# The first pair of W_in chunks of blocks 1 and 2 in seven products of half the depth

## The chip, the cores and the metric

The kernel runs on one core of one Trainium2 chip. The metric is device time in microseconds (us) of one execution, from the first to the last instruction of the core and what lies around them. Engines are named as in the profile: PE is TensorE's matmul, PEld its weight load, DVE is VectorE, ACT is ScalarE, POOL is GpSimd, SP is the queue that issues DMAs.

## The reference

Attention over 16 heads of 576 positions with a cumulative bias, a gated layer with RMS norm, and a second layer. The change lies in the second layer, cut here to what matters:

```python
def _moe2_ref(x, w_in, w_out):            # x: 1152 x 512, w_in: 512 x 2048, w_out: 2048 x 512
    h = x @ w_in
    sp = np.where(h > 20.0, h, np.log1p(np.exp(np.minimum(h, 20.0))))
    g = h * np.tanh(sp)                   # Mish
    return (g @ w_out)
```

## The kernel before

The 1152 tokens are three blocks (0, 1, 2) of 384 columns. Each fp32 operand is split into a high and a low part (`split_pair`: ScalarE copies the high part, VectorE subtracts it to get the low one), and each product is three passes (`PASS`) over these parts. `xh` and `xl` hold the two parts of x, four chunks of 128 rows each.

The 2048 columns of `w_in` are 16 chunks in eight pairs, g = 0 to 7. For one block and one pair there are two ways to compute h:

- **plain**, `h2_mm(b, g)`: two chunks, four row chunks, three passes, 24 matmuls of 384 columns into one pair of PSUM banks (`banksS`, two such pairs exist). Then `mish(b, g)` on ScalarE writes the tile `u`, `mish_split(b, g)` splits it into one half of the tile `glb`, and `out_mm(b, g)` multiplies by `w_out` (18 matmuls of 512 columns), adding up over g.
- **seven products**, `strassen(g, gaps)`: blocks 1 and 2 together. Strassen's scheme (in Winograd's form) takes seven products of half the depth (`product`, six matmuls each) in place of eight, 42 matmuls in place of 48. It needs sums of quarters of x, which are made once (`t_sums(1)` to `t_sums(4)`, split by `t_split`), and sums of quarters of the pair's weights, made for each g (`s_restore` adds high and low parts into a tile c, `s_sums` does four additions in it, `s_hi` on ScalarE and `s_lo` on VectorE split it). The seven products are, in order: a (needs no sum), b (needs `s_lo` and x sum 2), c (x sum 3), d (x sum 1), a again, c again (x sum 4), d again. The last three add onto the PSUM bank of a first one, after `add` has read it. `gaps` holds work that is written between the products.

The program's order on each engine is the order of the calls; each engine works strictly in that order. Block 0 goes plainly for all g, in a loop in which `out_mm(0, g - 2)` follows `h2_mm(0, g)`, and each step ends in two calls of `w_tick`. A `w_tick` decodes one tile of packed fp64 weights into high and low parts: loads through SP into tiles `r0` to `r3`, three operations on ScalarE, three on VectorE; a load can start when the tile four places earlier has been decoded.

After the loop pair 0 of blocks 1 and 2 goes plainly, `h2_mm(2, 0)` and `h2_mm(1, 0)`, around `out_mm(0, 7)`; pairs 1 to 7 go by `strassen`, each followed by `out_mm(1, g - 1)`. Three orders matter for what waits on what: `mish_split(0, g)` writes half g % 2 of `glb`, which `out_mm(0, g - 2)` reads; x's sum 1 and 2 are written over block 0's part of `xh` and `xl`, sum 3 over block 2's, sum 4 into half 0 of `glb`; sums and weights share the tiles `r0` to `r3`, `mm`, `ring4` and `ring8` by tag. The order after the loop:

```python
    out_mm(0, NG - 2)
    mish_split(0, NG - 1)
    t_split(4)
    s_restore(1)
    s_sums(1)
    h2_mm(2, 0)
```

Of the kernel before, what the change touches and what calls it, by code (L numbers as in the profile page):

```python
# [7 lines left out]
F32 = mybir.dt.float32  # L8
# [4 lines left out]
ALU = mybir.AluOpType  # L13
# [29 lines left out]
def tile_kernel(ctx: ExitStack, tc: tile.TileContext, kq, qq, v, s, w1, w2, rms_g, out):  # L43
# [10 lines left out]
    def sbt(shape, dt, tag, name):  # L54
        return sb.tile(shape, dt, tag=tag, name=name)
# [352 lines left out]
    def w_tick():  # L408

        n = done["c"]  # L410
        if n >= NUW or not free(seq[n]):
            return
        w_loads(LIM[0])
        done["t"] += 1
        ready = done["b"] > n
        if ready:
            w_hi(n)
        else:
            w_tops(n)
        for m in range(done["b"], min(n + 2, done["a"])):  # L420
            w_b(m)
            done["b"] = m + 1
        if n < done["b"]:
            w_c(n, not ready)
            done["c"] = n + 1
        if ready:
            w_tops(n)
        w_loads(LIM[0])
# [278 lines left out]

        add(o, quarter(0, c, b).bitcast(F32), quarter(1, c, b).bitcast(F32))

    def split_pair(h, l, src):  # L710
        nc.scalar.copy(out=h, in_=src)  # L711
        nc.vector.tensor_tensor(out=l, in0=src, in1=h.bitcast(F32), op=ALU.subtract)  # L712

    def product(t, A, B, start):
        n = 0
# [121 lines left out]
    def h2_mm(b, g):  # L837
        t = banksS()
        h2_t[b, g] = t
        for x in range(2):  # L840
            w = unit2(2 * (2 * g + x))
            n = 0
            for c in range(KD):
                for a, r in PASS:
                    nc.tensor.matmul(t[:, x, 0:TB], w[:, a, 128 * c:128 * c + 128],  # L845
                                     xhl[r][:, c, TB * b:TB * b + TB], start=(n == 0), stop=(n == 11))
                    n += 1
# [4 lines left out]
    def pair(t):  # L852
        return t[:, 0:2 * TB].rearrange("p (x n) -> p x n", x=2)
# [3 lines left out]
    def u_at(b, g):  # L857

        if (b, g) in u_t:
            return u_t[b, g]  # L860
        if b == 2 and g > 3:
            if not ub:
                ub.append(sbt([128, 4, 2, TB], F32, "w11", "ub"))
            u_t[b, g] = ub[0][:, g - 4]
        else:
            tag = ("mm", "ring8", "ring6", "ring0")[g] if b == 2 else ("hA", "hB")[g % 2] if b else                 ("hA", "hB", "mm")[g % 3]
            u_t[b, g] = sbt([128, 2, TB], F32, tag, "u")
        return u_t[b, g]

    def mish(b, g):  # L870
        nc.scalar.activation(out=u_at(b, g), in_=h2_t.pop((b, g))[:, :, 0:TB], func=ACTF.Mish)

    def mish_split(b, g):
        if not glb:
            glb.append(sbt([128, 2, 2, 2, TB], F32R, "w6", "glb"))
        g2_t[b, g] = gl = glb[0][:, g % 2 if b == 0 else (g + 1) % 2 if b == 2 else g < NG - 1]
        split_pair(gl[:, 0], gl[:, 1], u_t.pop((b, g)))
# [18 lines left out]
    def out_evac(b):  # L896
        for tt in range(TB // 128):
            if b == 0 and tt < 2:
                if not ob:
                    ob.append(sbt([128, 2, 512], F32, "r0", "osb"))  # L900
                t = ob[0][:, tt]
            else:
                t = sbt([128, 512], F32, f"r{(2 * b + tt) % 4}" if b else "hB", "osb")
            rows = slice(b * TB + 128 * tt, b * TB + 128 * tt + 128)

            cols = (slice(0, 256), slice(256, 512)) if (b, tt) == (NB - 1, 2) else (slice(0, 512),)
            for n, cs in enumerate(cols):
                if (tt + n) % 2 == 0:
                    nc.scalar.copy(out=t[:, cs], in_=o_t[b][tt][:, cs])
                else:  # L910
                    nc.vector.tensor_copy(out=t[:, cs], in_=o_t[b][tt][:, cs])
                nc.sync.dma_start(out=out[rows, cs], in_=t[:, cs])
# [3 lines left out]
    def t_sums(n):  # L916

        if n == 0:
            tq[0] = pair(sbt([128, 896], F32, "mm", "t0"))
        o = tq[0]  # L920
        if n:
            tq[n] = t = pair(sbt([128, 1024], F32, ("r2", "r3", "r0", "r1")[n - 1], f"t{n}"))
        if n == 0:
            restore(o, 0, 2)
        elif n == 1:
            restore(t, 0, 1)
            add(t, o, t, ALU.subtract)
        elif n == 2:
            restore(t, 1, 2)
        elif n == 3:  # L930
            add(t, tq[2], o, ALU.subtract)
            add(tq[2], tq[2], tq[1], ALU.subtract)
        else:
            restore(o, 1, 1)
            add(t, o, tq[2], ALU.subtract)

    def t_split(n):
        tsum[n] = ((quarter(0, 0, 0), quarter(1, 0, 0)), (quarter(0, 1, 0), quarter(1, 1, 0)),
                   (quarter(0, 0, 2), quarter(1, 0, 2)), (glb[0][:, 0, 0], glb[0][:, 0, 1]))[n - 1]
        split_pair(*tsum[n], tq[n])  # L940

    def s_restore(g):

        c_t[g] = sbt([128, 1024], F32, "r1", "c")
        for x in range(2):
            w = unit2(4 * g + 2 * x).bitcast(F32)
            add(c_t[g][:, 512 * x:512 * x + 512], w[:, 0], w[:, 1])

    def s_sums(g):

        a11, a12, a21, a22 = (c_t[g][:, 256 * n:256 * n + 256] for n in range(4))
        for o, x, y, op in ((a22, a21, a22, ALU.add), (a21, a11, a21, ALU.subtract),
                            (a11, a22, a11, ALU.subtract), (a12, a12, a11, ALU.subtract)):
            add(o, x, y, op)

    def s_hi(g):
        s_t[g] = [sbt([128, 1024], F32R, t, f"s_{t}") for t in (("r0", "ring4"), ("r2", "r3"))[g % 2]]
        nc.scalar.copy(out=s_t[g][0], in_=c_t[g])

    def s_lo(g):  # L960
        h, l = s_t[g]
        add(l, c_t.pop(g), h.bitcast(F32), ALU.subtract)

    def strassen(g, gaps):

        w1_, w2_ = unit2(4 * g), unit2(4 * g + 2)
        s2, s4, s3, s1 = ([t[:, 256 * n:256 * n + 256] for t in s_t[g]] for n in range(4))
        a11, a12, a22 = ([w[:, a, o:o + 256] for a in range(2)] for w, o in ((w1_, 0), (w1_, 256), (w2_, 256)))
        x = {(c, b): (quarter(0, c, b), quarter(1, c, b)) for c, b in ((0, 1), (1, 1), (1, 2))}
        u1, u2 = u_at(1, g), u_at(2, g)  # L970
        p, q = u2[:, 0], u2[:, 1]
        a, b, c = (psT.tile([128, 512], F32, tag="T", name=n)[:, 0:TB] for n in ("pa", "pb", "pc"))
        d = psX.tile([128, 512], F32, tag="X", name="pd")[:, 0:TB]
        product(a, a11, x[0, 1], True)
        nc.scalar.copy(out=p, in_=a)
        gaps[0]()
        product(b, s2, tsum[2], True)
        add(p, p, b)
        gaps[1]()
        product(c, s3, tsum[3], True)  # L980
        add(q, p, c)
        gaps[2]()
        product(d, s1, tsum[1], True)
        add(q, q, d)
        gaps[3]()
        product(a, a12, x[1, 1], False)
        nc.scalar.activation(out=u1[:, 0], in_=a, func=ACTF.Mish)
        gaps[4]()
        product(c, a22, tsum[4], False)
        add(u1[:, 1], p, c)  # L990
        nc.scalar.activation(out=u1[:, 1], in_=u1[:, 1], func=ACTF.Mish)
        gaps[5]()
        product(d, s4, x[1, 2], False)
        add(p, p, d)
        nc.scalar.activation(out=u2, in_=u2, func=ACTF.Mish)
# [185 lines left out]
    for g in range(1, NG):  # L1181
        h2_mm(0, g)
        mish_split(0, g - 1)
        mish(0, g)
        if g >= 2:
            out_mm(0, g - 2)
        w_tick()
        w_tick()
        if NG - 2 <= g:
            t_sums(g - NG + 2)  # L1190
    for n in (2, 3, 4):
        t_sums(n)
    for n in (2, 1):
        t_split(n)
    out_mm(0, NG - 2)
    mish_split(0, NG - 1)
    t_split(4)
    s_restore(1)
    s_sums(1)
    h2_mm(2, 0)  # L1200
    mish(2, 0)
    s_hi(1)
    s_lo(1)
    t_split(3)
    out_mm(0, NG - 1)
    out_evac(0)
    s_restore(2)
    h2_mm(1, 0)
    mish(1, 0)
    s_sums(2)  # L1210

    def doing(*fs):
        def run():
# [1 line left out]
                f(*args)  # L1215
        return run

    for g in range(1, NG):
        gaps = [nothing] * 6
        gaps[3] = doing((mish_split, 1, g - 1))  # L1220
        if g == 1:
            gaps[5] = doing((s_hi, g + 1))
        elif g + 1 < NG:
            gaps[0] = doing((s_hi, g + 1), (s_lo, g + 1))
        strassen(g, gaps)
        if g == 1:
            s_lo(g + 1)
        out_mm(1, g - 1)
        if g + 2 < NG:
            s_restore(g + 2)  # L1230
            s_sums(g + 2)
# [54 lines left out]
```

## Time and profile before

| | us |
|---|---|
| runs, median of 3 (lowest to highest) | 538.53 (534.33 to 539.4) |
| profiled execution, time | 532.69 |
| profiled execution, span | 530.9 |
| PE busy | 519.4 (98%) |
| DVE busy | 358.6 (68%) |
| ACT busy | 303.9 (57%) |
| POOL busy | 56.3 (11%) |

The span is the time from the first to the last instruction in the profiled execution; its time has 1.79 us more around that. Busy shares are means over the whole span. A matmul's duration in the profile overlaps the next one's; the pace from one start to the next is shorter than the duration.

### The profile page before, as it was taken

To read this page: it belongs to the slowest core of one execution; us is meant where nothing else is said; L and a number is where in the kernel's file an instruction comes from. 1 tells how busy PE (TensorE), PEld (TensorE's weight loads), DVE (VectorE), ACT (ScalarE), POOL (GpSimd) and SP (SyncE) were. 2 spreads that over 40 slices of the span, in tenths; PEclk is the share of its full clock that TensorE was granted. 3 is DMA by queue.
4 is the path that set the end of the run, shared out by engine and by line. 5 is a ranking of instruction groups with operands and counts; after the bars stand their busy time and mean duration, and the time that the engine had idled before them with its cause. 6 is when DMAs were issued, how large, how long until landed. Compare 5 with 4: busy or idle time off the path is not lost.

```text
span 530.9 us, 7988 instructions
## 1 busy us (share of the span) xinstructions
PE 519.4 (98%) x2948; PEld 469.7 (88%) x2948; DVE 358.6 (68%) x742; ACT 303.9 (57%) x650; POOL 56.3 (11%) x71
## 2 busy tenths in 40 slices
PE   8899999999999999999999999999999999999997
PEld 4677776688999999999999999999889999999885
DVE  7899999767977676575667666376578667653321
ACT  5777997863465566566478777575634433333211
POOL 6246656300000000000000000000000000000000
PEclk8899999999999999999999999999999999999999
DMA  9998995212004343435055634255101000000101
GB/s 227 272 234 232 248 250 133 81 60 99 12 30 129 103 138 113 154 119 165 34 166 163 187 89 151 79 160 154 45 0 60 0 1 0 2 0 1 59 1 59
DMA packets 18782, 55.90 MB, mean 105 GB/s; under 512 B 2348, under 2 KB 2604, under 8 KB 18716
## 3 DMA queue, kind: packets, MB, share of 16 engines
q1 hardware_dynamic: 13520, 42.04, 25.2%
q0 software_dynamic: 3712, 9.70, 9.0%
q10 hardware_dynamic: 1512, 3.66, 2.6%
q8 instruction: 23, 0.38, 0.3%
q14 instruction: 15, 0.12, 0.1%
HBM read 52.73 MB, written 2.66 MB: 104 GB/s over the span
## 4 chain that ended last, share of the span: by engine, by line
PE 92%; DVE 3%; ACT 1%; DMA 1%; issue 1%; POOL 0%; ACTq 0%; DVEq 0%; POOLq 0%
PE o L891 12%; PE gv L676 12%; PE y L821 9%; PE gv L845 8%; PE gv L694 8%; PE gv L891 6%; PE pa L718 5%; PE pd L718 5%; PE pc L718 5%; PE gv L821 5%; PE xa L552 5%; PE tp L514 4%; PE pb L718 2%; PE sc L466 2%; PE sc L467 2%; DMA w<-in_qq_dram 1%
## 5 line engine op out<-in xcount | busy, mean ns | idle before, releaser
L676 PE MATMUL gv<-xh,wring 128*128 128x384 f32 x256 | 67.1, 338 | 0.2 <-DVE h_w L685 0.2
L344 DVE SCALAR_TENSOR_TENSOR r<-r 128x512 int32<-128x512 int32 x68 | 47.4, 703 | 11.4 <-ACT r L337 8.4
L821 PE MATMUL y<-hhl,w 128*128 128x384 f32 x288 | 50.2, 334 | 0.0
L821 PEld LDWEIGHTS y<-hhl,w 128*128 128x128 f32 x288 | 49.9, 188 | 0.0
L676 PEld LDWEIGHTS gv<-xh,wring 128*128 128x128 f32 x256 | 46.4, 188 | 0.5 <-DVE h_w L685 0.3
L326 ACT ACTIVATE r<-r 128x512 int32<-128x512 uint8 x61 | 41.8, 685 | 8.0 <-DMA r<-in_w_dram 8.0
L498 ACT ACTIVATE px<-sc,cst 128x384 f32<-128x384 f32 (+2 forms) x80 | 41.3, 529 | 6.2 <-DVE cst L491 5.8
L676 PE MATMUL gv<-xl,wring 128*128 128x384 f32 x128 | 43.0, 336 | 0.0
L694 PE MATMUL gv<-xh,wring 128*128 128x384 f32 x160 | 41.6, 336 | 0.0
L337 ACT ACTIVATE r<-r 128x512 f32<-128x512 f32 x57 | 38.4, 673 | 0.0
L491 DVE CUSTOM_DVE_ANT_0 sc<-sc,xtm 128x384 f32<-128x384 f32 (+4 forms) x72 | 34.6, 500 | 3.3 <-PE sc L467 1.5
L514 PE MATMUL tp<-cst,px 128*128 128x128 f32 (+1 forms) x200 | 30.5, 282 | 2.3 <-DVE xl L635 1.4
L712 DVE TENSOR_TENSOR glb<-u,glb 128x768 fp32r<-128x768 f32 x20 | 19.1, 955 | 18.2 <-ACT glb L711 18.2
L514 PEld LDWEIGHTS tp<-cst,px 128*128 128x128 f32 (+1 forms) x200 | 23.8, 143 | 7.3 <-DVE xl L635 1.9
L552 PE MATMUL xa<-aw,px 128*64 128x320 f32 (+3 forms) x192 | 29.6, 377 | 0.3 <-DMA px<-in_v_dram 0.3
L804 DVE TENSOR_TENSOR hhl<-h_w,hhl 128x384 fp32r<-128x384 f32 x30 | 16.5, 557 | 18.7 <-ACT hhl L803 18.7
L694 PEld LDWEIGHTS gv<-xh,wring 128*128 128x128 f32 x160 | 29.0, 188 | 0.0
L891 PE MATMUL o<-wt,glb 128*128 128x512 f32 x108 | 26.9, 390 | 0.0
L694 PE MATMUL gv<-xl,wring 128*128 128x384 f32 x80 | 26.9, 336 | 0.0
L891 PE MATMUL o<-w,glb 128*128 128x512 f32 x108 | 26.5, 390 | 0.0
L821 PE MATMUL gv<-hhl,w 128*128 128x384 f32 x144 | 25.1, 334 | 0.0
L821 PEld LDWEIGHTS gv<-hhl,w 128*128 128x128 f32 x144 | 25.0, 188 | 0.0
(271 smaller groups left out, 1244.3 us busy)
## 6 DMA issues: line engine op xcount, KB each, us to landing
r<-in_w_dram SPq DMA_DIRECT2D x66, 512.0 KB, 4.0
w<-in_kq_dram POOLq DMA_DIRECT2D x7, 576.0 KB, 6.3
w<-in_qq_dram POOLq DMA_DIRECT2D x7, 576.0 KB, 7.0
out_dram<-osb SPq DMA_DIRECT2D x8, 256.0 KB, 2.1
px<-in_v_dram SPq DMA_DIRECT2D x5, 320.0 KB
r<-in_w_dram ACTq DMA_DIRECT2D x2, 512.0 KB, 4.4
px<-in_v_dram ACTq DMA_DIRECT2D x3, 320.0 KB
raw_hA<-in_kq_dram SPq DMA_DIRECT2D x3, 288.0 KB
```

What stands on the lines that cost most here:

```text
L326: nc.scalar.activation(out=low, in_=low.bitcast(U8)[:, :, 3], func=ACTF.Copy, scale=1 / 32, bias=-15.5 / 32)
L337: nc.scalar.activation(out=top, in_=top, func=ACTF.Prelu, scale=2.0 ** -112, alpha=-2.0 ** 32)
L344: nc.vector.scalar_tensor_tensor(out=low, in0=top, scalar=3, in1=low, op0=ALU.logical_shift_left, op1=ALU.bitwise_or)
L498: nc.scalar.activation(out=pv, in_=sv, func=ACTF.Exp, bias=sbias[:, c + x:c + x + 1], scale=-1.0, accum_out=ssum[:, sc:sc + 1])
L514: nc.tensor.transpose(t[0:rows, o - a:o - a + 128], P[pos[i] % 2][:, o:min(e, o + 128)], ident)
L552: nc.tensor.matmul(o, V[z][0:rows, c, ds], r, start=(c == 0), stop=(c == (1, 4)[part]))
L676: nc.tensor.matmul(t[:, g, 0:TB], w[:, a, 128 * c:128 * c + 128], xhl[r][:, c, TB * b:TB * b + TB], start=(n == 0), stop=(n == 11))
L694: nc.tensor.matmul(t[:, g, 0:TB], w[:, a, 128 * c:128 * c + 128], xhl[r][:, c, TB * b:TB * b + TB], start=(n == 0), stop=(n == 11))
L718: nc.tensor.matmul(t, A[a][:, 128 * c:128 * c + 128], B[r][:, c], start=(start and n == 0), stop=(n == 5), skip_group_check=True)
L821: nc.tensor.matmul(y_t[b][d], w[:, a, 128 * d:128 * d + 128], hhl[:, r], start=(f == FY[0] and y == 0), stop=(f == FY[-1] and y == 2))
L845: nc.tensor.matmul(t[:, x, 0:TB], w[:, a, 128 * c:128 * c + 128], xhl[r][:, c, TB * b:TB * b + TB], start=(n == 0), stop=(n == 11))
L891: nc.tensor.matmul(o_t[b][tt], gl[:, r, x, 128 * tt:128 * tt + 128], w[:, a], start=(g == 0 and x == 0 and y == 0), stop=(g == NG - 1 and ...
```

## The change

Pair 0 of blocks 1 and 2 goes by `strassen(0, ...)` too; `h2_mm(2, 0)`, `h2_mm(1, 0)` and their two `mish` calls go. For this:

- The steps 1 to 7 of block 0's loop call `w_tick` 2, 3, 2, 3, 2, 1 and 0 times in place of twice each. `t_sums(0)` to `t_sums(2)` are written at the end of step 6, `t_sums(3)` and `t_split(3)` within step 7, with `t_split(3)`'s subtraction on GpSimd.
- `s_restore(0)` and `s_sums(0)` follow the loop, then `mish_split(0, 7)`, `t_split(2)`, `t_split(1)`, `s_hi(0)`, `t_sums(4)`, `s_lo(0)`, then `out_mm(0, 6)`, `t_split(4)`, and `strassen(0)`. Its gaps hold `s_restore(1)`, `s_sums(1)` and `s_hi(1)`; `s_lo(1)`, `out_mm(0, 7)` and `out_evac(0)` follow.
- For g = 0 `strassen` takes its first three PSUM banks from the two `banksS` pairs, since the three `psT` banks hold block 0's output sums.
- `strassen(1)` has `s_restore(2)` in its last gap (it had `s_hi(2)`); `s_sums(2)`, `s_hi(2)` and `s_lo(2)` follow it.
- Tiles are given out anew: the split weight sums of even g lie in `r2` and `r3`, of odd g in `r0` and `ring8`; x's sum 4 lies in `r0` behind sum 3; the tile `u` of block 2's pair 1 in `ring4`; the first output tile of block 0 in `r1`.

```diff
--- before.py
+++ after.py
@@ -707,9 +707,9 @@
 
         add(o, quarter(0, c, b).bitcast(F32), quarter(1, c, b).bitcast(F32))
 
-    def split_pair(h, l, src):
+    def split_pair(h, l, src, eng=nc.vector):
         nc.scalar.copy(out=h, in_=src)
-        nc.vector.tensor_tensor(out=l, in0=src, in1=h.bitcast(F32), op=ALU.subtract)
+        eng.tensor_tensor(out=l, in0=src, in1=h.bitcast(F32), op=ALU.subtract)
 
     def product(t, A, B, start):
         n = 0
@@ -863,7 +863,7 @@
                 ub.append(sbt([128, 4, 2, TB], F32, "w11", "ub"))
             u_t[b, g] = ub[0][:, g - 4]
         else:
-            tag = ("mm", "ring8", "ring6", "ring0")[g] if b == 2 else ("hA", "hB")[g % 2] if b else                 ("hA", "hB", "mm")[g % 3]
+            tag = ("mm", "ring4", "ring6", "ring0")[g] if b == 2 else ("hA", "hB")[g % 2] if b else                 ("hA", "hB", "mm")[g % 3]
             u_t[b, g] = sbt([128, 2, TB], F32, tag, "u")
         return u_t[b, g]
 
@@ -897,7 +897,7 @@
         for tt in range(TB // 128):
             if b == 0 and tt < 2:
                 if not ob:
-                    ob.append(sbt([128, 2, 512], F32, "r0", "osb"))
+                    ob.append(sbt([128, 2, 512], F32, "r1", "osb"))
                 t = ob[0][:, tt]
             else:
                 t = sbt([128, 512], F32, f"r{(2 * b + tt) % 4}" if b else "hB", "osb")
@@ -919,7 +919,7 @@
             tq[0] = pair(sbt([128, 896], F32, "mm", "t0"))
         o = tq[0]
         if n:
-            tq[n] = t = pair(sbt([128, 1024], F32, ("r2", "r3", "r0", "r1")[n - 1], f"t{n}"))
+            tq[n] = t = pair(sbt([128, 1024], F32, ("r2", "r3", "r0", "r0")[n - 1], f"t{n}"))
         if n == 0:
             restore(o, 0, 2)
         elif n == 1:
@@ -934,10 +934,10 @@
             restore(o, 1, 1)
             add(t, o, tq[2], ALU.subtract)
 
-    def t_split(n):
+    def t_split(n, eng=nc.vector):
         tsum[n] = ((quarter(0, 0, 0), quarter(1, 0, 0)), (quarter(0, 1, 0), quarter(1, 1, 0)),
                    (quarter(0, 0, 2), quarter(1, 0, 2)), (glb[0][:, 0, 0], glb[0][:, 0, 1]))[n - 1]
-        split_pair(*tsum[n], tq[n])
+        split_pair(*tsum[n], tq[n], eng)
 
     def s_restore(g):
 
@@ -954,7 +954,7 @@
             add(o, x, y, op)
 
     def s_hi(g):
-        s_t[g] = [sbt([128, 1024], F32R, t, f"s_{t}") for t in (("r0", "ring4"), ("r2", "r3"))[g % 2]]
+        s_t[g] = [sbt([128, 1024], F32R, t, f"s_{t}") for t in (("r2", "r3"), ("r0", "ring8"))[g % 2]]
         nc.scalar.copy(out=s_t[g][0], in_=c_t[g])
 
     def s_lo(g):
@@ -969,7 +969,11 @@
         x = {(c, b): (quarter(0, c, b), quarter(1, c, b)) for c, b in ((0, 1), (1, 1), (1, 2))}
         u1, u2 = u_at(1, g), u_at(2, g)
         p, q = u2[:, 0], u2[:, 1]
-        a, b, c = (psT.tile([128, 512], F32, tag="T", name=n)[:, 0:TB] for n in ("pa", "pb", "pc"))
+        if g:
+            a, b, c = (psT.tile([128, 512], F32, tag="T", name=n)[:, 0:TB] for n in ("pa", "pb", "pc"))
+        else:
+            pab, pc = banksS(), banksS()
+            a, b, c = pab[:, 0, 0:TB], pab[:, 1, 0:TB], pc[:, 0, 0:TB]
         d = psX.tile([128, 512], F32, tag="X", name="pd")[:, 0:TB]
         product(a, a11, x[0, 1], True)
         nc.scalar.copy(out=p, in_=a)
@@ -1181,33 +1185,27 @@
     for g in range(1, NG):
         h2_mm(0, g)
         mish_split(0, g - 1)
+        if g == NG - 1:
+            t_sums(3)
+            t_split(3, nc.gpsimd)
         mish(0, g)
         if g >= 2:
             out_mm(0, g - 2)
-        w_tick()
-        w_tick()
-        if NG - 2 <= g:
-            t_sums(g - NG + 2)
-    for n in (2, 3, 4):
-        t_sums(n)
-    for n in (2, 1):
-        t_split(n)
+        for _ in range((0, 2, 3, 2, 3, 2, 1, 0)[g]):
+            w_tick()
+        if g == NG - 2:
+            for n in range(3):
+                t_sums(n)
+    s_restore(0)
+    s_sums(0)
+    mish_split(0, NG - 1)
+    t_split(2)
+    t_split(1)
+    s_hi(0)
+    t_sums(4)
+    s_lo(0)
     out_mm(0, NG - 2)
-    mish_split(0, NG - 1)
     t_split(4)
-    s_restore(1)
-    s_sums(1)
-    h2_mm(2, 0)
-    mish(2, 0)
-    s_hi(1)
-    s_lo(1)
-    t_split(3)
-    out_mm(0, NG - 1)
-    out_evac(0)
-    s_restore(2)
-    h2_mm(1, 0)
-    mish(1, 0)
-    s_sums(2)
 
     def doing(*fs):
         def run():
@@ -1215,15 +1213,21 @@
                 f(*args)
         return run
 
+    strassen(0, [nothing, doing((s_restore, 1)), nothing, doing((s_sums, 1)), nothing, doing((s_hi, 1))])
+    s_lo(1)
+    out_mm(0, NG - 1)
+    out_evac(0)
     for g in range(1, NG):
         gaps = [nothing] * 6
         gaps[3] = doing((mish_split, 1, g - 1))
         if g == 1:
-            gaps[5] = doing((s_hi, g + 1))
+            gaps[5] = doing((s_restore, g + 1))
         elif g + 1 < NG:
             gaps[0] = doing((s_hi, g + 1), (s_lo, g + 1))
         strassen(g, gaps)
         if g == 1:
+            s_sums(g + 1)
+            s_hi(g + 1)
             s_lo(g + 1)
         out_mm(1, g - 1)
         if g + 2 < NG:
```

## Rows read from the trace of the kernel before

**Rows 1.** Chain that ended last, share of the span by engine.

```profile
PE 92%; DVE 3%; ACT 1%; DMA 1%; issue 1%; POOL 0%; ACTq 0%; DVEq 0%; POOLq 0%
```

**Rows 2.** The same chain, 364 to 427 us: start us, duration us, what.

```profile
364.33 4.12 PE o L891 x18
...
389.25 8.20 PE o L891 x36
397.46 4.20 PE gv L845 x24
...
405.77 4.19 PE gv L845 x24
...
417.30 4.20 PE gv L891 x18
...
426.71 1.05 PE pc L718 x6
```

**Rows 3.** Stretches of the span: busy us of each engine, granted clock, DMA.

```profile
core 0: us, PE busy (x) PEld busy (x) DVE busy (x) ACT busy (x) POOL busy (x), PEclk, DMA share, GB/s
0.00:20.00 20.00, 16.19 (x61) 10.23 (x61) 15.07 (x36) 12.05 (x33) 11.99 (x28) 0.83 1.05 254
...
389.00:410.00 21.00, 21.00 (x106) 18.82 (x105) 17.71 (x24) 8.06 (x11) 0.00 (x0) 1.00 0.03 12
...
12.00:14.00 2.00, 1.65 (x8) 1.10 (x8) 1.93 (x9) 2.00 (x7) 0.00 (x0) 0.50 1.33 302
...
86.00:96.00 10.00, 8.02 (x58) 6.12 (x57) 9.67 (x26) 7.31 (x23) 7.12 (x8) 1.00 0.16 39
```

**Rows 4.** VectorE, 350 to 398 us: start us, us, instruction, idle before it.

```profile
350.61 0.69 DVE L360 TENSOR_TENSOR w<-r,w 128x512 fp32r<-128x512 f32 x1
...
369.42 0.96 DVE L712 TENSOR_TENSOR glb<-u,glb 128x768 fp32r<-128x768 f32 x1 [0.51 <-ACT glb L711]
...
382.37 0.69 DVE L360 TENSOR_TENSOR w<-r,w 128x512 fp32r<-128x512 f32 x1 [2.35 <-ACT w L351]
...
390.67 0.69 DVE L360 TENSOR_TENSOR wt<-r,wt 128x512 fp32r<-128x512 f32 x1 [3.42 <-ACT wt L351]
...
395.99 0.95 DVE L704 TENSOR_TENSOR t<-xh,xl 128x768 f32<-128x768 f32 x1
396.98 0.96 DVE L704 TENSOR_TENSOR t<-t,t 128x768 f32<-128x768 f32 x1
397.85 1.82 DVE L712 TENSOR_TENSOR xl<-t,xh 128x768 fp32r<-128x768 f32 x2
```

**Rows 5.** DMA issues of the weights: KB each, median us from issue to landing.

```profile
r<-in_w_dram SPq DMA_DIRECT2D x66, 512.0 KB, 4.0
```

**Rows 6.** ScalarE in order of time, 368 to 418 us.

```profile
368.55 0.84 ACT L711 CAST glb<-u 128x768 fp32r<-128x768 f32 x1
...
417.30 1.03 ACT L958 CAST s_r<-c 128x1024 fp32r<-128x1024 f32 x1
```

**Rows 7.** GpSimd's groups by line and form: busy us, mean ns.

```profile
L360 POOL TENSOR_TENSOR wring<-r,wring 128x512 fp32r<-128x512 f32 x7 | 9.1, 1297 | 23.0 <-ACT wring L351 16.4 <-issue 6.5
```

**Rows 8.** VectorE in order of time, 416 to 426 us.

```profile
416.28 0.56 DVE L704 TENSOR_TENSOR u<-u,pc 128x384 f32<-128x384 f32 x1 [0.66 <-PE pc L718]
...
418.36 1.23 DVE L704 TENSOR_TENSOR s_ring<-c,s_r 128x1024 fp32r<-128x1024 f32 x1 [0.47 <-ACT s_r L958]
419.62 1.29 DVE L704 TENSOR_TENSOR c<-wt 128x512 f32<-128x512 f32 x2
420.95 1.80 DVE L704 TENSOR_TENSOR c<-c 128x256 f32<-128x256 f32 x4
424.05 1.23 DVE L704 TENSOR_TENSOR s_r<-c,s_r 128x1024 fp32r<-128x1024 f32 x1 [1.29 <-ACT s_r L958]
425.19 0.55 DVE L704 TENSOR_TENSOR u<-u,pb 128x384 f32<-128x384 f32 x1
425.84 0.56 DVE L704 TENSOR_TENSOR u<-u,pc 128x384 f32<-128x384 f32 x1
```

## The prediction

> **What bounds the kernel now.** I read the chain of work that ended last first: TensorE holds 92% of the span [rows 1]. In order of time it is TensorE alone around the change: from 364.33 us to past 426.71 us each piece starts where the last one ended, with nothing between [rows 2]. The table by stretches agrees: in 389 to 410 us, where the edit lies, TensorE is busy 21.00 of 21.00 us at a granted clock of 1.00, while VectorE works 17.71 us and ScalarE 8.06 us [rows 3]. So two things count: how many matmuls are issued, and whether a result of VectorE or ScalarE now comes later than TensorE asks for it. VectorE is 84% busy there and the change puts more work before a deadline, so I followed its queue step by step.
>
> **The matmuls.** The two plain stages `h2_mm(2, 0)` and `h2_mm(1, 0)` go: 4.20 and 4.19 us, 24 matmuls each [rows 2]. `strassen(0)` comes: 42 matmuls of the same shape; its twin `strassen(1)` lasts from 405.77 + 4.19 = 409.96 to 417.30, 7.34 us [rows 2]. Gain 8.39 - 7.34 = 1.05 us, which is six matmuls, and it is the whole gain: no other work of TensorE changes.
>
> **Decoding.** The ticks of the loop become 2, 3, 2, 3, 2, 1, 0 in place of two each. With two each, the last step has one weight subtraction only, at 390.67 [rows 4], so its second tick is empty: 13 are needed and 13 are kept, and nothing is left undecoded. A third tick in one step asks for a weight tile whose load starts only when the first tick of that step has finished, for example after the subtraction at 350.61; a load takes 4.0 us to land [rows 4, 5]. ScalarE then stands at that load until some 355.3. Behind it in ScalarE's queue are `mish_split(0, 2)` and `mish(0, 3)`. With its remaining work ScalarE would come to them at about 357 and 358. The first is needed by `out_mm(0, 2)` at 364.33, the second frees the PSUM pair of `h2_mm(0, 5)`, which begins when `out_mm(0, 2)` ends, at 364.33 + 4.12 = 368.45 [rows 2]. Seven and ten microseconds of TensorE's own work hide a delay of about 3, so I put it at nothing; without that cover it would cost those 3 us, in each of the two steps with three ticks.
>
> **The moved sums and the first new wait.** VectorE is free after the last tick's subtraction, which moves up by one step, to 382.37 [rows 4], so `t_sums(0)` to `t_sums(3)`, `s_restore(0)` and `s_sums(0)` and `mish_split(0, 6)` run from 383 to about 392.7, ahead of need. `t_split(3)`'s subtraction goes to GpSimd. The trace has GpSimd's subtraction for 128x512 at 1.30 us [rows 7], so for 768 columns 1.95 us is my estimate, 2.9 if it is slowed by half; `t_sums(4)`, which takes over its tile `r0`, writes at 397.9. That is hidden with 5 us to spare.
>
> Then the chain that can't be early. `mish_split(0, 7)` overwrites the half of `glb` that `out_mm(0, 5)` reads, and the splits of the sums are now queued behind it on both engines. `out_mm(0, 5)` and `out_mm(0, 6)` run from 389.25 for 8.20 us [rows 2], so the first ends at 393.35. Elsewhere such a copy starts 0.10 us after the reader's end (368.45 to 368.55 [rows 2, 6]) and its subtraction 0.87 us later (369.42 [rows 4]). So:
> - copy of `mish_split(0, 7)` at 393.45, subtraction at 394.32; the subtractions of `t_split(2)` and `t_split(1)` follow at VectorE's pace of 0.87 us (two of 0.95 take 1.82 [rows 4]) and the last ends at 397.0;
> - `t_sums(4)`: its two additions take 0.99 and 0.87 us to the next start (395.99, 396.98, 397.85 [rows 4]), so `s_lo(0)` starts at 398.8. `s_hi(0)`, for which tile `r2` comes free at 397.0, needs 1.06 us to let it start (417.30 to 418.36 [rows 6, 8]) and isn't the later one;
> - `s_lo(0)` lasts 1.23 us [rows 8]: it ends at 400.0.
>
> TensorE finishes `out_mm(0, 6)` at 397.46 and the first product, which needs no sum, at 398.51. The second product reads `s_lo(0)`'s result in its third matmul; two matmuls of 0.17 us carry it to 398.86. It waits until 400.05: **1.2 us**. If the whole product waits it is 1.55; if the splits overlap better than I have it, 0.9. What follows keeps up: `t_split(4)` is done near 401.0 and is wanted by the sixth product, past 404; `out_evac(0)` stands between `out_mm(0, 7)` and `strassen(1)` with no stage of cover any more, but its banks are freed in the order in which `strassen(1)` takes them, one product apart.
>
> **The second new wait.** Before, `s_restore(2)` and `s_sums(2)` were finished ahead of `strassen(1)` and only `s_lo(2)` came behind it (418.36), then `s_restore(3)`, `s_sums(3)`, `s_lo(3)` and two additions up to 426.40; the sixth product of `strassen(2)`, which overwrites what the second addition reads, starts at 426.71 [rows 2, 8]. The margin is 0.3 us. After, `s_restore(2)` is in the last gap of `strassen(1)` and `s_sums(2)`, `s_hi(2)`, `s_lo(2)` come behind it, so six operations enter this same line. On the clock of before, by the starts of [rows 8]:
> - the addition at 416.28 ends at 416.8; `s_restore(2)` takes 1.33 (419.62 to 420.95), to 418.1; the addition of the last product 0.65, to 418.8; `s_sums(2)` 1.80, to 420.6;
> - `s_hi(2)` 1.06 on ScalarE and a handover of 0.05: `s_lo(2)` at 421.7, ending at 422.9. `strassen(2)` needs it in the third matmul of its second product, at 421.50 + 1.40 = 422.9 (421.50 is 417.30 + 4.20 [rows 2]): just met;
> - 1.26 to the next start (418.36 to 419.62), then `s_restore(3)` 1.33, `s_sums(3)` 1.80: 426.1; `s_hi(3)` and handover 1.1: `s_lo(3)` at 427.2; 1.14 (424.05 to 425.19) and 0.65 (425.19 to 425.84) to the second addition, which ends 0.56 later, at 429.55.
>
> The sixth product then starts at 429.6 in place of 426.71: **2.9 us**. If the pair of `s_restore(2)` slips in ahead of the addition without delay it is 2.1; if ScalarE's Mish gets in the way of `s_hi`, 3.3. Later steps are not touched: their sums have a whole stage in hand again.
>
> **The sum.** -1.05 + 1.2 + 2.9 = +3.05 us. The profiled execution has a span of 530.9 us and a time of 532.69; after: span 533.9, time 535.7. The runs shown have a median of 538.53 (534.33 to 539.4), so the profiled one is 1.1% below it; the same step on the median gives **541.5 us**, 0.6% more, which is less than the 1% that a measurement of this kernel can tell from no change.
>
> **What TensorE's clock may add.** The trace shows 1.00 in 86 to 96 us, although TensorE is idle for 2 of those 10 us in several pieces [rows 3]; no row shows one idle stretch of 2.9 us. At the start the clock was 0.50 (1.2 GHz) in 12 to 14 us and 0.83 over the first 20 us [rows 3]. 0.83 means 6.8 us at the lower level, so 3.4 us lost. So a fall of that kind would be worth 3.4 us. The Trainium skill, "TensorE: Matmul & The Clock Gate", section "Why this matters for your kernels", asks that TensorE isn't left idle for long between bursts of matmuls, since the clock then goes back to its lower level. By that rule the second wait could cost more than its own length; no row here shows whether it does.
>
> **The rivals.**
> - *No wait shows* (0.13): the VectorE lines overlap better than I add them up, and only the six matmuls are left: 538.53 - 1.05 = 537.5. For it: VectorE had 3.3 us without work in 389 to 410. Against: the idle time lies before the release of `glb`, where it doesn't help.
> - *One wait only* (0.17): the second alone gives 540.4, the first alone 538.7. The first hangs on an order of three queues, the second on one line of operations whose margin is 0.3 us; the second is the surer.
> - *The clock falls in the second wait* (0.07): another 3.4 us, so 541.5 + 3.4 = 544.9, 1.2% slower. It decides from the point where one idle stretch of 2.9 us, longer than any that the rows show, makes the clock fall. Against it: the matmuls before and behind are dense, and scattered idle time of 2 in 10 us did nothing [rows 3]. The skill's rule named above is this mechanism.
> - *The third tick reaches TensorE* (0.03): 3 us in each of two steps, 547.5; only if the cover of ten microseconds isn't there.
>
> **How the numbers follow.** Both waits: 0.60. The range runs from the case without waits, 537.5, less 1 for the scatter of the runs shown, to the clock case: 536.5 to 545.0. Faster by over 1% would need -5.4 us, for which no term exists: 0.03, for scatter. Slower by over 1%: the clock and tick cases, and the forecast with its waits at the upper ends (+3.85) and scatter: 0.15. Within 1%: 0.82.
>
> **What would show it.** In the chain of the changed kernel, seven `product` groups between `out_mm(0, 6)` and `out_mm(0, 7)`; a gap of about 1.2 us in the second, with VectorE's `s_lo(0)` as releaser, and of about 2.9 us ahead of the sixth product of `strassen(2)`, with an addition at `add`'s line as releaser; TensorE's matmuls six fewer; granted clock 1.00 there. I am wrong if the chain is TensorE without a gap (then the time falls by 1 us), or if a gap sits elsewhere, at `out_evac(0)` or in the loop's third ticks.

## The result and the profile after

Measured together, the kernel before has a median of 535.37 us and the changed kernel one of 541.8 us (22 runs each): ratio 1.0119, 95% interval 1.0094 to 1.0145. The ratio leaves out runs more than 1.5% above the fastest of their kernel, one of each. The change costs 6.4 us where I forecast 3.05, and it is 1.2% slower, where I had given 0.15 to more than 1%. The time named, 541.5, was met by luck: it stood on a median of three runs that was 3 us too high, and the step that I added to it was 3 us too small.

The page of the profiled execution (time 539.59 us), its parts 1 and 4:

```profile
span 537.8 us, 7995 instructions
PE 520.0 (97%) x2942; PEld 469.4 (87%) x2942; DVE 364.2 (68%) x753; ACT 305.6 (57%) x653; POOL 58.9 (11%) x72
...
PE 87%; DVE 5%; DMA 3%; ACT 2%; issue 2%; POOL 0%; ACTq 0%; DVEq 0%; POOLq 0%
```

Six matmuls fewer (2942), as the diff says, but TensorE's share of the chain is down from 92% [rows 1] to 87%, and VectorE's is up from 3% to 5%. What TensorE waited for from 340 us on, as total us, number of waits and longest wait (the kernel before has no such row in this stretch):

```profile
PE pc L718 <- DVE u L704: 2.5, 1, 2.5
PE gv L718 <- ACT u L979: 1.8, 1, 1.8
```

The chain in order of time answers to [rows 2]:

```profile
350.62 4.20 PE o L891 x18
...
392.26 4.14 PE o L891 x18
...
402.07 0.83 ACT glb L711
402.90 0.39 ACT u L979
403.29 0.04 issue
403.33 2.36 PE gv L718 x12
...
409.87 4.12 PE o L891 x18
413.99 1.04 PE pa L718 x6
...
432.65 0.56 DVE u L704
433.21 0.04 issue
433.26 1.31 PE pc L718 x6
434.57 1.04 PE pd L718 x6
435.61 4.20 PE gv L891 x18
```

The reader is to see two places where the chain leaves TensorE: ahead of 403.33, product b of `strassen(0)`, and ahead of 433.26, the sixth product of `strassen(2)`. They are the two places of the forecast. The releaser of the first isn't the one forecast: it is ScalarE's copy of product a, not VectorE's `s_lo(0)`. TensorE's own rows there:

```profile
403.33 0.45 PE L718 MATMUL gv<-xh,s_r 128*128 128x384 f32 x1 [1.81 <-ACT u L979]
...
433.26 1.31 PE L718 MATMUL pc<-glb,wt 128*128 128x384 f32 x6 [2.52 <-DVE u L704]
```

To compare executions I cut the span at two starts, `out_mm(0, 0)` and the first product of `strassen(1)`. Ahead of the first cut all engines have the same instructions as before. **A** is the stretch between the cuts, with the loop and the first new wait; **B** goes from the second cut to the end of the span. All in us, one profile each; the last column says behind which wait the granted clock was at 0.50 for some us.

| run | first cut | A | B | clock at 0.50 |
|---|---|---|---|---|
| before | 347.45 | 62.35 | 121.10 | none |
| before_again | 351.44 | 62.35 | 121.11 | none |
| after | 350.46 | 63.37 | 123.97 | none |
| after_again | 351.37 | 63.35 | 125.48 | second |
| after_third | 350.32 | 64.93 | 125.45 | both |
| split7_late | 350.76 | 62.16 | 125.48 | second |
| sums2_early | 351.45 | 63.36 | 121.19 | none |
| split3_dve | 349.01 | 63.28 | 125.31 | second |
| after_fill | 350.63 | 63.35 | 123.92 | none |
| after_fill2 | 347.83 | 64.92 | 123.95 | first |
| all_early | 352.12 | 62.13 | 121.15 | none |
| all_early_banks | 350.36 | 61.31 | 121.13 | none |

Without the clock the change costs (63.37 - 62.35) + (123.97 - 121.10) = 1.02 + 2.87 = 3.9 us; with it, up to (64.93 + 125.45) - (62.35 + 121.10) = 6.9 us.

A wait costs more than the idle time in its row. Against `all_early_banks`, which has neither wait, the first costs 63.37 - 61.31 = 2.06 us and the second 123.97 - 121.13 = 2.84, where the rows give 1.81 and 2.52. Most of the rest is at the restart: behind the second wait six matmuls take 1.31 us in place of 1.04, behind the first twelve take 2.36 in place of 2.09, at a granted clock of 1.00 (the rows are above, those of the clock below).

### The profile page after: what moved, and what is told of

It reads as the page before. It is cut to its first block, busy times and chain, and to the rows that moved or that the text cites. A ratio compares the mean times of both kernels' runs of the same rounds, so it can differ in the third digit from the quotient of the medians.

```text
span 537.8 us, 7995 instructions
## 1 busy us (share of the span) xinstructions
PE 520.0 (97%) x2942; PEld 469.4 (87%) x2942; DVE 364.2 (68%) x753; ACT 305.6 (57%) x653; POOL 58.9 (11%) x72
## 4 chain that ended last, share of the span: by engine, by line
PE 87%; DVE 5%; DMA 3%; ACT 2%; issue 2%; POOL 0%; ACTq 0%; DVEq 0%; POOLq 0%
PE gv L676 12%; PE o L891 12%; PE y L821 9%; PE gv L694 8%; PE gv L845 6%; PE gv L891 5%; PE pd L718 5%; PE gv L821 5%; PE pc L718 5%; PE pa L718 4%; PE xa L552 4%; PE tp L514 4%; PE pb L718 2%; PE sc L466 2%; DMA w<-in_qq_dram 2%; DMA raw_hB<-in_kq_dram 2%
## 5 line engine op out<-in xcount | busy, mean ns | idle before, releaser
L491 DVE CUSTOM_DVE_ANT_0 sc<-sc,xtm 128x384 f32<-128x384 f32 (+4 forms) x72 | 34.5, 499 | 3.0 <-PE sc L467 1.9
L712 POOL TENSOR_TENSOR xl<-t,xh 128x768 fp32r<-128x768 f32 x1 | 2.4, 2356 | 276.9 <-ACT xh L711 276.9
L466 PE MATMUL sc<-w 128*128 128x384 f32 (+1 forms) x64 | 24.5, 394 | 2.0 <-DMA w<-in_qq_dram 1.9
```

The lines of the kernel that those rows point to most:

```text
L466: nc.tensor.matmul(o, QA[z][:, qs], KA[z][:, ks], start=(n != 1), stop=False)
```

## The experiments

**Is the start part of the change?** The two first profiles differ by 3.0 us ahead of the edit already. `before_again` is the kernel before, unedited.

> The kernel before, unchanged, against itself. It asks how much of the difference between the two profiled executions lies ahead of the edit: the fourth load of q (line 146, second issue) landed at 10.5 us in the first profile of before and at 13.1 us in that of after, and out_mm(0, 0) began at 347.6 against 350.6 us, with the same instructions on every engine up to there. Theory: that start is chance from execution to execution, so here the ratio is 1.000 within 0.003, and the load may land anywhere from 10.5 to 13.1 us. Rival: the start belongs to the program, so that the kernel before lands it at 10.5 us every time, and the kernel after at 13.1.

Ratio 0.9983 (0.9954 to 1.0012). The load in question landed at 11.7 us (a DMA of the chain, start and duration):

```profile
3.79 7.91 DMA w<-in_qq_dram
```

The first cut lies at 351.44 here and at 347.45 in the first profile, with one and the same program; over all twelve profiles it goes from 347.45 to 352.12. So the start differs from execution to execution of one program, and the first profile of before had the earliest of all.

**The first wait.** `split7_late` moves one call of the changed kernel:

```diff
     s_sums(0)
-    mish_split(0, NG - 1)
     t_split(2)
...
     out_mm(0, NG - 2)
+    mish_split(0, NG - 1)
     t_split(4)
```

> The changed kernel with mish_split(0, 7) moved behind s_lo(0) and out_mm(0, 6). Theory: the first wait (1.8 us) comes from the splits of the sums standing behind that copy, which waits for out_mm(0, 5). With it gone VectorE goes on at once after s_sums(0): s_lo(0) ends about 1.1 us earlier and the first wait falls to 0.6 to 0.9 us; the second wait stays at 2.5 us; ratio to before about 1.010. Rival: the wait is set by the copy of product a out of PSUM, whose pair b shares, so it stays at 1.8 us.

The wait fell from 1.8 to 0.6 us and A from 63.37 to 62.16; ratio 1.0062 (1.002 to 1.0104), where I expected about 1.010. So two thirds of the first wait came from the queue behind `out_mm(0, 5)`. The 0.6 us left have ScalarE's copy of product a as releaser again:

```profile
402.43 0.45 PE L718 MATMUL gv<-xh,s_r 128*128 128x384 f32 x1 [0.60 <-ACT u L979]
```

**The second wait.** `sums2_early` puts the sums of pair 2 back ahead of `strassen(1)`:

```diff
-                    ob.append(sbt([128, 2, 512], F32, "r1", "osb"))
+                    ob.append(sbt([128, 2, 512], F32, "r2", "osb"))
...
     out_evac(0)
+    s_restore(2)
+    s_sums(2)
     for g in range(1, NG):
...
-            gaps[5] = doing((s_restore, g + 1))
+            gaps[5] = doing((s_hi, g + 1))
...
         if g == 1:
-            s_sums(g + 1)
-            s_hi(g + 1)
             s_lo(g + 1)
```

> The changed kernel with s_restore(2) and s_sums(2) ahead of strassen(1), as in the kernel before, and s_hi(2) in its last gap; the first output tile of block 0 goes to r2 in place of r1 to make that possible. Theory: the second wait (2.5 us ahead of the sixth product of strassen(2)) is gone and nothing takes its place; the first stays at 1.8 us. From the start of strassen(1) to the end of the span 121.0 us, as before (120.9), in place of 123.8; ratio to before about 1.007. Rival: VectorE is late there anyway, behind out_evac(0), and some of the wait comes back ahead of strassen(1): 122 us or more.

No wait is left in `strassen(2)`, B is 121.19 us, A unchanged; ratio 1.0047 (1.0009 to 1.0085). The theory holds, the rival doesn't.

**GpSimd's part.** `split3_dve` calls `t_split(3)` in place of `t_split(3, nc.gpsimd)`.

> The changed kernel with t_split(3)'s subtraction on VectorE. In the changed kernel the two additions of s_restore(0) took 2.94 us while GpSimd did that subtraction (2.36 us), where such a pair took 1.29 us elsewhere. Theory: they compete; here the pair takes 1.3 us, the subtraction 0.95 us on VectorE, and the first wait stays at 1.8 us, since it hangs on out_mm(0, 5). Rival: the pair waits for something else, and stays near 2.9 us; or the first wait shrinks with it by 1 us or more.

It was run once, so it has no ratio. VectorE's rows for the two additions of `s_restore(0)` (start, duration of both), first in the changed kernel, then GpSimd's row there, then VectorE's in `split3_dve`:

```profile
392.31 2.94 DVE L704 TENSOR_TENSOR c<-wring 128x512 f32<-128x512 f32 x2
```
```profile
392.35 2.36 POOL L712 TENSOR_TENSOR xl<-t,xh 128x768 fp32r<-128x768 f32 x1 [276.92 <-ACT xh L711]
```
```profile
391.73 1.28 DVE L704 TENSOR_TENSOR c<-wring 128x512 f32<-128x512 f32 x2
```

Beside GpSimd's subtraction VectorE's pair took 2.94 us, without it 1.28. All of the difference is in the second addition (2.34 us in place of 0.68), which ended 0.55 us behind GpSimd's subtraction; the seven profiles with that subtraction on GpSimd agree, and so do the three without. The first wait stayed at 1.7 us all the same, so this was hidden.

**The clock.** In two of these variants, `split7_late` and `split3_dve`, B is 1.3 to 1.5 us longer than in the changed kernel with the same second wait; the difference stood in the granted clock. `after_again` and `after_third` are the changed kernel, unedited. `after_fill` and `after_fill2` add matmuls that nobody reads to the second wait:

```diff
         gaps[4]()
+        if g == 2:
+            for _ in range(13):
+                nc.tensor.matmul(spare[0][:, 0:TB], a11[0][:, 0:128], x[0, 1][0][:, 0], start=True, stop=True)
```

> The changed kernel once more. Two variants of it showed a granted clock of 0.50 for about three microseconds behind the second wait (2.5 us of idle TensorE), where the first profile of the changed kernel showed 1.00. Theory: the clock falls in some executions of the same program and not in others; here the ratio is again 1.010 to 1.013, which is more than the 3.9 us (0.7%) that the first pair of profiles shows behind the start of out_mm(0, 0). Rival: the fall belongs to the variants alone, and the rest of the 1.2% is the start: then the clock is 1.00 and the ratio may be anything from 1.006 up.

> The changed kernel with 13 more matmuls of 384 columns in the second wait, into a PSUM bank that nobody reads, ahead of the sixth product of strassen(2); they take 2.26 us of the 2.5 us. Theory: the wait makes the clock fall in most executions, which costs up to 1.7 us; busy TensorE keeps it at 1.00, so that added work makes the kernel no slower, and the ratio falls by 0.001 to 0.003 against the changed kernel in the same batch. From the start of strassen(1) to the end of the span 123.8 us, as in the first profile of the changed kernel. Rival: the clock has no part in the median; the ratio is that of the changed kernel, or above it if the extra matmuls don't fit.

> The changed kernel a third time, beside after_fill2 on the same chip. Of four profiles with an empty second wait so far, three showed a granted clock of 0.50 behind it and 1.5 us more from strassen(1) to the end. Theory: it falls in most executions; ratio 1.010 to 1.012. Rival: the clock is chance that has nothing to do with the wait.

> The changed kernel with the 13 idle matmuls in the second wait, again: the first time the profile showed 1.00, as the first profile of the unfilled kernel did. Theory: 1.00 and 123.9 us from strassen(1) to the end once more, and a ratio 0.001 to 0.003 below that of after_third. Rival: 0.50 here too, about 125.5 us, and the same ratio.

Stretches of the changed kernel, first profile (us, busy us of each engine and their counts, granted clock third from the end):

```profile
401.00:403.00 2.00, 0.53 (x3) 0.20 (x2) 1.88 (x2) 1.06 (x3) 0.00 (x0) 1.00 0.00 0
403.00:404.00 1.00, 0.67 (x4) 0.67 (x5) 1.00 (x2) 0.28 (x1) 0.00 (x0) 1.00 0.00 0
432.00:433.00 1.00, 0.00 (x0) 0.00 (x0) 0.90 (x3) 0.00 (x0) 0.00 (x0) 1.00 0.00 0
433.00:437.00 4.00, 3.74 (x19) 3.47 (x20) 3.45 (x7) 1.29 (x2) 0.00 (x0) 1.00 0.00 0
```

The same stretches of the same program in `after_third`:

```profile
402.00:403.00 1.00, 0.00 (x0) 0.00 (x0) 1.00 (x1) 1.00 (x2) 0.00 (x0) 1.00 0.00 0
403.00:404.00 1.00, 0.81 (x4) 0.81 (x5) 1.00 (x2) 0.14 (x1) 0.00 (x0) 0.92 0.00 0
404.00:407.00 3.00, 3.00 (x11) 3.00 (x11) 1.89 (x5) 0.00 (x0) 0.00 (x0) 0.50 0.00 0
...
434.00:435.00 1.00, 0.33 (x1) 0.33 (x2) 0.83 (x2) 0.00 (x0) 0.00 (x0) 0.78 0.00 0
435.00:437.00 2.00, 2.00 (x7) 2.00 (x7) 1.15 (x3) 0.00 (x0) 0.00 (x0) 0.50 0.00 0
```

`split3_dve`, around its second wait, which ends at 431.72:

```profile
431.00:432.00 1.00, 0.28 (x1) 0.28 (x2) 0.79 (x3) 0.00 (x0) 0.00 (x0) 0.68 0.00 0
432.00:433.00 1.00, 1.00 (x4) 1.00 (x5) 1.00 (x2) 0.00 (x0) 0.00 (x0) 0.50 0.00 0
```

The clock falls to 0.50 (1.2 GHz) about where the wait ends: 0.4 us ahead of the first matmul in `split3_dve` (0.68 in the us from 431 means 0.64 us at the lower level), 0.6 us behind it at the first wait of `after_third`, 1.5 us behind it in `split7_late`. In `after_third` 11 matmuls run in the 3 us from 404, where 17 fit at a pace of 0.174 us.

Behind the second wait, left empty, it fell in four of five profiles and B grew by 125.45 - 123.97 = 1.5 us (1.3 in `split3_dve`). Behind the first, 1.7 or 1.8 us long, it fell in two of seven and A grew by 64.93 - 63.37 = 1.6 us.

In all twelve profiles the clock is at 1.00 from 40 us to the last matmul, but for these falls. Ahead of that, at 34.5 to 35.0 us, it falls in `split7_late`, `after_fill` and `all_early_banks`, each time behind 1.4 to 1.5 us without matmuls; five others with 1.2 to 1.6 us there keep 1.00.

With the second wait filled but for 0.3 us it stayed at 1.00 there in both profiles, and B was 123.92 and 123.95, although 2.3 us of matmuls had been added. In the ratios this doesn't show: 1.0111 (1.0069 to 1.0154) against 1.0102 (1.0054 to 1.015) in one batch, 1.01 (1.0057 to 1.0144) against 1.0104 (1.0052 to 1.0156) in the other. The medians lie lower with the wait filled, 539.81 against 542.05 and 539.01 against 541.35, but these are 4 and 6 runs each. The step that I expected, 0.001 to 0.003, is smaller than these intervals, and two profiles don't settle that the filling is what kept the clock up.

**Both orders mended.** `all_early` has the edits of `split7_late`, `sums2_early` and `split3_dve`, and sums earlier in the loop:

```diff
-        if g == NG - 1:
-            t_sums(3)
-            t_split(3, nc.gpsimd)
+        if g == NG - 2:
+            for n in range(3):
+                t_sums(n)
+        if g == NG - 1:
+            t_split(3)
         mish(0, g)
...
         if g == NG - 2:
-            for n in range(3):
-                t_sums(n)
-    s_restore(0)
-    s_sums(0)
+            t_sums(3)
+            s_restore(0)
+            s_sums(0)
```

`all_early_banks` gives out the PSUM banks of `strassen(0)` differently as well:

```diff
-            pab, pc = banksS(), banksS()
-            a, b, c = pab[:, 0, 0:TB], pab[:, 1, 0:TB], pc[:, 0, 0:TB]
-        d = psX.tile([128, 512], F32, tag="X", name="pd")[:, 0:TB]
+            pbd, pc = banksS(), banksS()
+            b, d, c = pbd[:, 0, 0:TB], pbd[:, 1, 0:TB], pc[:, 0, 0:TB]
+        px1 = psX.tile([128, 512], F32, tag="X", name="pd")[:, 0:TB]
+        if g:
+            d = px1
+        else:
+            a = px1
```

> The changed kernel with both orders mended: t_sums(0) to t_sums(2) ahead of step 6's ticks, t_sums(3), s_restore(0), s_sums(0) behind them, t_split(3) on VectorE, mish_split(0, 7) behind s_lo(0), and s_restore(2), s_sums(2) ahead of strassen(1) with the first output tile in r2. Theory: s_lo(0) is done before out_mm(0, 6) ends, so what is left of the first wait is the copy of product a out of the PSUM pair that b shares: 0.5 us; the second wait is gone. From out_mm(0, 0) to the end 183.45 - 1.05 + 0.5 = 182.9 us. Rival for the pair: b waits for nothing, and it is 182.4.

> As all_early, with the four PSUM banks of strassen(0) given out so that a pair holds b and d, which aren't used one behind the other; a has a bank of its own. Theory: no wait of TensorE is left, the six matmuls fewer are all that remains: 182.4 us from out_mm(0, 0) to the end, 1.05 us less than before, ratio 0.998 within 0.003. Rival: another wait comes up in strassen(0) or behind it (the sums of pair 1, the output copies), 183 us or more, ratio 1.000 or above.

`all_early`, run once: 62.13 + 121.15 = 183.3 us where I expected 182.9, with one wait, at the same place and of the same releaser as in the changed kernel. It costs 62.13 - 61.31 = 0.82 us against `all_early_banks`, again some 0.25 more than its row:

```profile
403.76 0.45 PE L718 MATMUL gv<-xh,s_r 128*128 128x384 f32 x1 [0.57 <-ACT u L979]
```

In `all_early_banks` TensorE waits nowhere behind 140 us, and the chain runs through:

```profile
395.83 4.53 PE o L891 x20
400.36 1.06 PE pd L718 x6
401.43 3.15 PE gv L718 x18
404.57 1.04 PE pd L718 x6
405.62 2.09 PE gv L718 x12
407.71 4.12 PE o L891 x18
411.83 1.04 PE pa L718 x6
```

A + B = 182.44 us, 1.01 us less than before: the six matmuls. Ratio 0.9978 (0.9948 to 1.0008). It is the fastest version here, but the interval takes in 1.

## Why the prediction was right or wrong

**The matmuls: right.** Gain 1.05 us forecast; 1.01 us shown by `all_early_banks`, where nothing else is in the way.

**The first wait: right in its place and its main cause, too small.** Forecast 1.2 us in product b's third matmul, with 1.55 if the whole product waits; measured 1.8 in the row and 2.06 in the stretch A, and the whole product waits. This term was mis-sized by 0.9 us: to the 1.55 come 0.25 us of VectorE's line and some 0.25 of restart. Three things were missed. The line behind `out_mm(0, 5)` took 0.25 us more than added up: from the copy of `mish_split(0, 7)` to the end of `s_lo(0)` 6.58 us by my sums (393.45 to 400.03), 6.83 here (396.48 to 403.31):

```profile
397.35 0.96 DVE L712 TENSOR_TENSOR glb<-u,glb 128x768 fp32r<-128x768 f32 x1 [0.25 <-ACT glb L711]
398.22 1.82 DVE L712 TENSOR_TENSOR xl<-t,xh 128x768 fp32r<-128x768 f32 x2
399.96 0.95 DVE L704 TENSOR_TENSOR t<-xh,xl 128x768 f32<-128x768 f32 x1
401.02 0.96 DVE L704 TENSOR_TENSOR t<-t,t 128x768 f32<-128x768 f32 x1
402.08 1.23 DVE L704 TENSOR_TENSOR s_r<-c,s_r 128x1024 fp32r<-128x1024 f32 x1
```

The two additions took 1.06 us each to the next start, where I had 0.99 and 0.87 from [rows 4]. And products a and b lie in one pair of PSUM banks, so that b's first matmul waits for ScalarE's copy of a (402.81 to 403.28), which is queued behind `t_split(4)`'s copy. `all_early` and `all_early_banks` show this wait alone: 0.57 us with the shared pair, none without. In the changed kernel `s_lo(0)`, the releaser that I named, ends at 403.31, as late as the copy; without the shared pair b's third matmul would still have waited for it, by these times. I gave the release of `glb` the whole of the wait; `split7_late` gives it 1.2 of the 1.8 us. And the restart, some 0.25 us behind the idle time, is in no term of the forecast.

**VectorE's idle time ahead of the release: shorter than I said.** GpSimd's subtraction took 2.36 us, inside my 1.95 to 2.9, but I had it beside VectorE at no cost, and VectorE's pair took 2.94 us in place of 1.28. The 0.25 us of idle time at 397.35 is what was left of my cover.

**The second wait: right in place, releaser and cost, the cost partly by luck.** Forecast 2.9 us; idle for 2.5, and 2.84 in the stretch B. The line was 0.4 us shorter than added up, and the restart that I had left out makes up most of it. VectorE's rows answer to [rows 8]:

```profile
421.97 0.55 DVE L704 TENSOR_TENSOR u<-u,pd 128x384 f32<-128x384 f32 x1
422.43 1.80 DVE L704 TENSOR_TENSOR c<-c 128x256 f32<-128x256 f32 x4
425.35 1.23 DVE L704 TENSOR_TENSOR s_r<-c,s_r 128x1024 fp32r<-128x1024 f32 x1 [1.12 <-ACT s_r L958]
426.61 1.29 DVE L704 TENSOR_TENSOR c<-wt 128x512 f32<-128x512 f32 x2
427.94 1.80 DVE L704 TENSOR_TENSOR c<-c 128x256 f32<-128x256 f32 x4
430.86 1.23 DVE L704 TENSOR_TENSOR s_ring<-c,s_r 128x1024 fp32r<-128x1024 f32 x1 [1.11 <-ACT s_r L958]
432.00 0.55 DVE L704 TENSOR_TENSOR u<-u,pb 128x384 f32<-128x384 f32 x1
432.65 0.55 DVE L704 TENSOR_TENSOR u<-u,pc 128x384 f32<-128x384 f32 x1
```

`s_sums(2)` starts 0.4 us earlier after the start of `strassen(1)` (422.43, less 413.99) than by my sums (418.8, less 409.96). The addition ahead of it took 0.46 us to the next start, not 0.65, and the pair of `s_restore(2)` 1.20 (420.77 to 421.97), not 1.33. From `s_sums(2)` on the line is as added up.

**The clock: the step that failed.** I made it a rival with a chance of 0.07, for one wait alone, since the matmuls around are dense. It fell in five of the eight profiles in which at least one of the two waits was left in full, in one of them behind both. Its price of 3.4 us was too high: 1.3 to 1.6 us a fall. The rule of the Trainium skill named in the prediction ("TensorE: Matmul & The Clock Gate", "Why this matters for your kernels") warns of idle gaps longer than these. The trace agrees with it on the kind of effect, with 0.50 in 404 to 407 us above, but shows it behind 1.7 to 2.5 us of idle TensorE and in some executions only. Without the clock the parts measured add up to -1.01 + 2.06 + 2.84 = 3.9 us, where I had 3.05; the rest of the 6.4 us is put down to the clock. Going by the profiles, my estimate of the mean cost is 3.9 + 1.6 x 2/7 + 1.5 x 4/5 = 5.6 us, inside the measured 5.0 to 7.8 (0.94% to 1.45% of 535.37). What the remaining 0.8 us would be, if it is real, stays open.

**What cost nothing, as forecast.** The third ticks: ScalarE waited up to 1.45 us for a load in such a step, and TensorE waited for nothing there. `out_evac(0)` without its stage of cover: `strassen(1)` starts at 413.99, where `out_mm(0, 7)` ends.

## What to carry to other kernels

When TensorE is the whole chain, a cheaper algorithm on it is worth only its matmuls, here 1 us, and each operand that it needs has a due time; add up the in-order queue that makes the operand from the last release that it can't get around (here the reader of a half tile), and put what waits for that release behind what doesn't. A wait of 2 us on TensorE should be priced with its restart (some 0.3 us here) and with its clock. With the wait filled with matmuls that nobody reads the clock stayed up in both profiles, but no time was gained that could be measured. Moving the sums gained 2.8 us in B (ratio 1.0047 in place of 1.0119).

## What the hardware showed that I had not expected

The same program, with the same waits, has its clock halved or not from one execution to the next: 2.5 us of idle TensorE were followed by 1.00 once and by 0.50 four times, 1.7 to 1.8 us by 1.00 five times and by 0.50 twice. Each fall cost 1.3 to 1.6 us.

VectorE's pair of additions, which read two tensors from SBUF, took 2.94 in place of 1.28 us beside a subtraction of GpSimd that does so too. That subtraction took 2.36 us; by the 1.30 us that GpSimd needs for 512 columns [rows 7] my estimate for it alone is 1.95, but no run shows it alone.
